# A leaky ReLU's maximum queued behind the attention's next row maximum, and a smaller TensorE budget for the dense layers in each attention cycle

## The chip, the cores and the metric

One core of a Trainium2 chip runs the whole program. The metric is the device time of one execution in microseconds (us); several runs are given with their median. TensorE is written PE, VectorE DVE, ScalarE ACT, GpSimd POOL and SyncE SP, as in the profile. PE multiplies and writes PSUM; DVE, ACT and POOL work elementwise; POOL does not read PSUM here. Each engine takes its instructions in the order in which the program lists them.

## The reference: what is computed

Attention over 8 batches and 8 heads of 576 positions with 64 features, followed by two dense layers with a leaky ReLU between them. In the attention a score further than tau below its row's maximum gets no weight:

```python
scores = scale * np.matmul(q, k.transpose(0, 1, 3, 2))
thresh = np.max(scores, axis=-1, keepdims=True) - tau
scores = np.where(scores >= thresh, scores, -1e9)
attn = np.exp(scores - np.max(scores, axis=-1, keepdims=True))
x = (attn / (attn.sum(-1, keepdims=True) + 1e-9)) @ v      # to 4608 tokens x 512
h = x @ w_in                                               # 512 -> 2048
g = np.maximum(h, 0.0) + alpha * np.minimum(h, 0.0)        # alpha: one per column
out = g @ w_out                                            # 2048 -> 512
```

## The kernel before, in words

**Attention.** Two heads make a pair, so there are 32 pairs; a pair's queries make nine units of 128 rows, so there are 288 units. The loop at L910 runs one cycle for each unit. In cycle i the engines work on units at different stages. The calls of one cycle, in the order in which they are issued (from cycle 52 on), are: `mask` of unit i (DVE, L461: compares with the threshold and multiplies the exponentials); `scores` of unit i+2 (PE, L426: four matmuls, eight for a pair's fifth unit); `lo_k` and `lo` of unit i-1 (DVE, L526: low parts of the transposes); `turn` and `turn_k` of unit i (PE, L470 and L486: transposes); then the dense layers' share (below); then all that is listed for this cycle in `soon` and `later` (preparations of q, k and v, the products with v at L573, their eviction, reciprocals, results); then a first-layer product, if the cycle has one; then `hi_k` and `hi` of unit i (ACT, L522: high parts of the transposes); and at last `rowmax` (DVE, L441) and `expo` (ACT, L449 and L454) of unit i+2. Engines follow this order by hand: the schedule of PE, ACT, DVE and POOL is manual, and only semaphores make one wait for another. The scores have two PSUM buffers, so `scores` of unit i+2 waits for the mask of unit i. The products with v of a pair fall into the sixth and seventh cycle of the pair and into the second and third of the next (L573).

**Dense layers.** Six of the sixteen column blocks of the hidden layer are done in groups of 256 tokens (18 groups), as soon as the tokens of a batch are there. A group is: a load of x (L200), its split into high and low part (ACT L206, POOL L207), six first-layer products (`layer1`, L219, 12 matmuls each, here "L1"), and 36 second-layer matmuls (`layer2`, L249, here "L2") into two accumulators. After an L1 in cycle i, cycle i+1 calls `prelu` from `later`: ACT copies the product with a sign (L232), DVE takes the maximum of that and slope times the product (L233, which reads PSUM again). Cycle i+2 calls `split_g` (POOL L242 cast, L243 difference). The finished accumulator is copied by ACT (L746) and stored by SP (L747).

How many of these go into a cycle is set by a budget in us, `Mlp.cycle`: what the attention uses of PE in this cycle (0.92, and more where the fifth unit's scores, an extra transpose or a product with v falls in) is taken from `CYCLE`; an L1 costs 1.31 and runs only in cycles without a product with v, an L2 costs 0.216:

```python
self.room = min(self.room, TH3) + CYCLE - used
...
elif slot and not HOLD[0] <= i - total < HOLD[1] and self.room > TH1 and ...:
    l1 = True
    self.room -= 1.31
while self.l2 and self.l2[0][0] <= i and ... and self.room > TH2:
    self.step_l2(i)
    self.room -= 0.216
```

The transposes, the products with v, the L1 products and the L2 accumulators share four PSUM buffers (pool `ps_m`, tag "pm").

**Behind the loop.** At cycle 297 the attention's memory is given back. What is left of the queued L2s runs, then the groups that are left, one after another, as `jobs`: `first_layer` (L1056) and `second_layer` (L1068), with `fetch_x` (L866) for their tokens. After that come the other ten column blocks by another method (from L1106 on: products at L1239 and L1417).

Of the kernel before, what the change touches and what calls it, by code (L numbers as in the profile page):

```python
# [15 lines left out]
AF = mybir.ActivationFunctionType  # L16
ALU = mybir.AluOpType
# [8 lines left out]
F1 = 6  # L26
G1 = 256
# [9 lines left out]
GB = 11  # L37
# [15 lines left out]
ACTO, SPLO, PUTO = 1, 2, 1  # L53
# [9 lines left out]
DEC0, DEC = -3, 3  # L63
DECO0, DECO = 16, 3
RDY = 13
CYCLE = 2.6
EW0, EW = 62, 10


# [12 lines left out]
def tile_masked_attention_moe(  # L82
# [11 lines left out]
    nc = tc.nc  # L94
# [14 lines left out]
    turn_sb = const.tile([P, NF], F32, name="turn_sb")  # L109
    tiny_sb = const.tile([P, NF], F32, name="tiny_sb")  # L110
    slope_sb = const.tile([P, NF], F32, name="slope_sb")
# [82 lines left out]
    def load_x(pool, t0, n, gn, bufs):  # L194
        xl = pool.tile([P, NCC, gn], F32R, tag="xl", name=f"xl{gn}_{t0}", bufs=bufs)
        t = t0
        while t < t0 + n:
            b, o = divmod(t, S)
            m = min(S - o, t0 + n - t)
            nc.sync.dma_start(f(xl[:, :, t - t0 : t - t0 + m]), xs[b][:, :, o : o + m].rearrange("c p t -> p c t"))  # L200
            t += m
        return xl

    def split_x(pool, xl, t0, n, gn, bufs):
        xh = pool.tile([P, NCC, gn], F32R, tag="xh", name=f"xh{gn}_{t0}", bufs=bufs)
        nc.scalar.activation(xh[:, :, :n], f(xl[:, :, :n]), AF.Copy)  # L206
        nc.gpsimd.tensor_tensor(xl[:, :, :n], f(xl[:, :, :n]), f(xh[:, :, :n]), op=ALU.subtract)  # L207
        return xh, xl

    def layer1(ps_m, fc, n, x, name):  # L210
        return layer1_into(ps_m.tile([P, 512], F32, tag="pm", name=f"ph{name}"), fc, n, x)
# [13 lines left out]
                )  # L225
        return ph

    def prelu(pool, gn, fc, n, ph, name, bufs):

        t = pool.tile([P, gn], F32, tag="pt", name=f"pt{name}", bufs=bufs)  # L230
        col = slice(fc, fc + 1)
        nc.scalar.activation(t[:, :n], ph[:, :n], AF.Copy, scale=turn_sb[:, col])  # L232
        nc.vector.scalar_tensor_tensor(  # L233
            t[:, :n], ph[:, :n], slope_sb[:, col], t[:, :n], op0=ALU.mult, op1=ALU.max
        )
        return t

    def split_g(g, t, n, eng=None):
        if eng is None:
            nc.scalar.activation(g[:, 0, :n], t[:, :n], AF.Copy)  # L240
        else:
            eng.tensor_copy(g[:, 0, :n], t[:, :n])  # L242
        nc.gpsimd.tensor_tensor(g[:, 1, :n], t[:, :n], f(g[:, 0, :n]), op=ALU.subtract)  # L243
# [7 lines left out]
    fcs1 = list(range(F1))  # L251
# [6 lines left out]
    mem = SimpleNamespace(mp1=None)  # L258
# [374 lines left out]
            nc.sync.dma_start(xs[self.b][self.hp], self.x)  # L633

    pairs = [Pair(pi) for pi in range(npairs)]
    soon, later = {}, {}

    def at_cycle(i, fn, *a):
        later.setdefault(i, []).append((fn, a))
# [5 lines left out]
    for p in pairs:  # L645
        o = 9 * p.pi
        n = o - 9
# [36 lines left out]
    class Mlp:  # L684
# [16 lines left out]
        def step_l1(self, i):  # L701
            gi, st, fi = self.l1.popleft()
            t0, n = groups1[gi]
            if fi is None:
                st["xr"] = load_x(mem.mp1, t0, n, G1, 1)
                at_cycle(i + XO, lambda: st.update(x=split_x(mem.mp1, st["xr"], t0, n, G1, 1)))
                self.gap = i + XO + 2
                return
            name = f"a{gi}_{fi}"
            self.live += 1  # L710
            ph = layer1(ps_m, fcs1[fi], n, st["x"], name)

            alone = i >= total

            def act(ph=ph):
                st[fi] = prelu(mem.mp1, G1, fcs1[fi], n, ph, name, 3)

            def spl():
                g = mem.mp1.tile([P, 2, G1], F32R, tag="g", name=f"g{name}", bufs=GB)
                split_g(g, st.pop(fi), n, None if alone else dict(p=nc.gpsimd, v=nc.vector).get(SPG))  # L720
                st["g"][fi] = g

            at_cycle(i + ACTO, act)
            at_cycle(i + SPLO, spl)
            if fi == F1 - 1:
                for o in range(0, n, P):
                    for fj in range(F1):
                        self.l2.extend((i + L2O, gi, st, o, fj, ti) for ti in range(3))
# [22 lines left out]
        def cycle(self, i, used, slot):  # L751

            self.room = min(self.room, TH3) + CYCLE - used
            l1 = False
            if self.l1 and i >= self.gap and self.live < GB:
                if self.l1[0][2] is None:
                    self.step_l1(i)
                elif slot and not HOLD[0] <= i - total < HOLD[1] and self.room > TH1 and ("i", fcs1[self.l1[0][2]]) in ready:
                    l1 = True
                    self.room -= 1.31  # L760
            while self.l2 and self.l2[0][0] <= i and self.l2[0][4] in self.l2[0][2]["g"] and ("o", fcs1[self.l2[0][4]]) in ready and self.room > TH2:
                self.step_l2(i)
                self.room -= 0.216
            return l1
# [5 lines left out]
    def unit(i):  # L770
        return (pairs[i // 9], i % 9) if 0 <= i < total else (None, 0)

    def do(i, name):
        p, u = unit(i)
        if p is not None:
            getattr(p, name)(u)
# [120 lines left out]
    with tc.manual_schedule(engines=ENGINES) if ENGINES else ExitStack():  # L897
# [12 lines left out]
        for i in range(-3, total + CLOSE):  # L910
            if i == -1:
                p.prep_vh()
                p.prep_vl()
            if i == SPC:
                sp.close()
                mem.mp1 = p1.enter_context(tc.tile_pool(name="mp1", bufs=1, side="right", reuse_waits="tile"))
            do(i, "mask")
            do(i + 2, "scores")
            ab = i < SW
            if not ab or i % 2 == 0:  # L920
                do(i - 1, "lo_k")
                do(i - 1, "lo")
            else:
                do(i + 1, "rowmax")
                do(i + 1, "expo")
            do(i, "turn")
            do(i, "turn_k")
            while nready < len(groups1) and sum(groups1[nready]) <= (i - RDY) // (9 * NPAIR) * S:
                mlp.ready(nready)
                nready += 1  # L930
            used = 0.92
            if unit(i + 2)[1] == 4:
                used += 0.49
            if unit(i)[1] in (1, 3, 4, 6, 8):
                used += 0.11
            used += busy.get(i, 0.0)
            if i >= total:
                used = 0.0
            l1 = mlp.cycle(i, used, i not in busy)
            for fn, a in soon.pop(i, []) + later.pop(i, []):  # L940
                fn(*a)
            if l1:
                mlp.step_l1(i)
            do(i, "hi_k")
            do(i, "hi")
            if ab and i % 2:
                do(i - 1, "lo_k")
                do(i - 1, "lo")
            if not ab or i % 2:
                do(i + 2, "rowmax")  # L950
                do(i + 2, "expo")

        i = total + CLOSE
        at.close()
        left = [ExitStack() for _ in range(7)]
        pool = lambda k, name, side: left[k].enter_context(tc.tile_pool(name=name, bufs=1, side=side, reuse_waits="tile"))
# [66 lines left out]
        jobs = []  # L1023
        for gi, st, fi in mlp.l1:
            if not jobs or jobs[-1].gi != gi:
                t0, n = groups1[gi]
# [4 lines left out]
        for gi in range(nready, len(groups1)):  # L1031
            t0, n = groups1[gi]
# [4 lines left out]
        def fetch(num):  # L1037
            if num < len(jobs) and not jobs[num].x:
                job = jobs[num]
                job.x = fetch_x(job.t0, job.n, i, 4, job.name)  # L1040
# [15 lines left out]
        def first_layer(job, j):  # L1056
            fc = fcs1[j]
            name = f"{job.name}_{fc}"
            while "x" not in job.x:
                cycle()  # L1060
            ph = ps_2.tile([P, 512], F32, tag="ph", name=f"ph{name}", bufs=4)
            layer1_into(ph, fc, job.n, job.x["x"])
            cycle()
            t = prelu(mem.mp1, G1, fc, job.n, ph, name, 3)
            job.g[j] = mem.mp1.tile([P, 2, G1], F32R, tag="g", name=f"g{name}", bufs=GB)
            split_g(job.g[j], t, job.n)

# [21 lines left out]
        pending = None  # L1089
        for num, job in enumerate(jobs):  # L1090
            fetch(num + 1)
            last = num == len(jobs) - 1
            for k, j in enumerate(job.todo):
                if k == 0 and num == 1 and pending.begun:
                    cycle()
                    second_layer(pending, mem.mp1)
                first_layer(job, j)
                if k == (GB - F1 - 1 if last else 0) and num > 0 and not (num == 1 and pending.begun):
                    second_layer(pending, mem.mp1)
            if not last:  # L1100
                pending = job


# [417 lines left out]
```

## Time and profile before

| | |
|---|---|
| median of three runs | 1427.89 us (1427.32 to 1430.94) |
| the profiled execution | 1431.79 us |
| its span, first to last instruction | 1429.6 us |
| PE clock granted, mean | 0.986 of full |
| busy share of the span: PE, DVE, ACT, POOL | 92%, 79%, 70%, 48% |

The span is what the views below are cut from. "Busy" of PE includes modelled ends of pipelined matmuls. A row of a timeline has the start (us from the span's start), the duration in us, the engine, the line, the operation, what it writes and reads, the shape, the number of merged instructions, and in brackets the idle time of the engine before it with what ended it.

### The profile page before, as it was taken

How to read it: one execution, taken by the hardware profiler on the slowest of the kernel's cores; microseconds unless marked ns; L12 is line 12 of the kernel's file. 1: busy time of each engine (PE TensorE's matmuls, PEld its weight loads, DVE VectorE, ACT ScalarE, POOL GpSimd, SP SyncE). 2: the span in 40 equal slices, each digit the busy share in tenths (PEclk: the TensorE clock that was granted, in tenths of full speed). 3: DMA queues.
4: the chain of work that ended last, by engine and by line, in shares of the span. 5: the costliest groups of instructions: out<-in, count | busy, mean ns of one | idle time of the engine just before them, and what ended most of it. 6: DMA issues, size and time to landing. Idle time of an engine off the chain costs nothing. (4 is left out here: it accounts for less than half of the span.)

```text
span 1429.6 us, 26323 instructions
## 1 busy us (share of the span) xinstructions
PE 1320.5 (92%) x8998; PEld 1224.3 (86%) x8998; DVE 1126.8 (79%) x2127; ACT 997.1 (70%) x2162; POOL 686.6 (48%) x865
## 2 busy tenths in 40 slices
PE   5988899999899899999999998999999999999998
PEld 4656888888788788888888987889999999999998
DVE  6888788888888788888888885546887758787785
ACT  6898788878888887878888885656676666333332
POOL 3775465465555555655555544756665554000000
PEclk9999899999999999999999999998999999999999
DMA  7645444543644644554454432335555465656552
GB/s 229 176 123 136 129 132 130 159 124 111 181 117 132 171 125 125 144 161 136 119 162 129 117 103 81 108 111 168 172 188 170 155 197 194 188 170 202 175 162 74
DMA packets 147765, 210.31 MB, mean 147 GB/s; under 512 B 16336, under 2 KB 91888, under 8 KB 147632
## 3 DMA queue, kind: packets, MB, share of 16 engines
q1 hardware_dynamic: 147632, 208.63, 49.8%
q8 instruction: 72, 1.18, 0.3%
q14 instruction: 61, 0.50, 0.1%
HBM read 111.75 MB, written 54.67 MB: 116 GB/s over the span
## 5 line engine op out<-in xcount | busy, mean ns | idle before, releaser
L441 DVE TENSOR_REDUCE nmx<-s 128x1 f32<-128x576 f32 x288 | 216.3, 751 | 62.7 <-PE s L426 60.1
L426 PE MATMUL s<-kh,qst 128*128 128x288 f32 x640 | 149.2, 323 | 86.6 <-DVE p L461 57.9
L449 ACT ACTIVATE p<-s,nmx 128x576 f32<-128x576 f32 x256 | 189.9, 742 | 43.2 <-DVE nmx L441 42.6
L461 DVE SCALAR_TENSOR_TENSOR p<-s,thr,p 128x576 f32<-128x576 f32 x256 | 206.9, 808 | 3.5 <-ACT thr L454 3.0
L426 PEld LDWEIGHTS s<-kh,qst 128*128 128x128 f32 x640 | 98.9, 192 | 127.7 <-issue 54.0
L470 PE MATMUL t<-ident,p 128*128 128x128 f32 x1024 | 156.7, 276 | 1.1 <-DVE p L461 1.1
L249 PE MATMUL acca<-wo,ga 128*128 128x512 f32 x504 | 147.3, 414 | 1.2 <-POOL ga L243 1.2
L219 PE MATMUL pha<-xh,wi 128*128 128x256 f32 x672 | 140.3, 292 | 2.1 <-DVE pta L233 1.7
L1239 PE MATMUL pX<-xh,wa 128*128 128x384 f32 x480 | 136.1, 343 | 6.4 <-DVE pZ L1279 3.9
L426 PE MATMUL s<-kl,qst 128*128 128x288 f32 x640 | 134.1, 300 | 0.0
L1417 PE MATMUL pX<-wb,gh 128*128 128x256 f32 x720 | 129.7, 282 | 0.0
L470 PEld LDWEIGHTS t<-ident,p 128*128 128x128 f32 x1024 | 127.8, 143 | 1.4 <-DVE p L461 1.3
L219 PEld LDWEIGHTS pha<-xh,wi 128*128 128x128 f32 x672 | 111.2, 193 | 6.0 <-DVE pta L233 4.0
L1417 PEld LDWEIGHTS pX<-wb,gh 128*128 128x128 f32 x720 | 111.6, 191 | 0.0
L573 PE MATMUL av<-eo,vst 128*128 128x322 f32 (+1 forms) x512 | 108.6, 335 | 0.0
L861 ACT ACTIVATE gh<-gr 128x1280 fp32r<-128x1280 f32 x45 | 57.4, 1275 | 71.4 <-PE pX L1417 42.7
L526 DVE TENSOR_TENSOR eo<-t,eo 128x512 fp32r<-128x512 f32 (+1 forms) x168 | 97.4, 593 | 10.1 <-ACT eo L522 9.6
L426 PEld LDWEIGHTS s<-kl,qst 128*128 128x128 f32 x640 | 102.8, 192 | 0.0
L1417 PE MATMUL pX<-wb,gl 128*128 128x256 f32 x360 | 101.6, 282 | 0.0
L249 PEld LDWEIGHTS acca<-wo,ga 128*128 128x128 f32 x504 | 89.1, 191 | 14.2 <-POOL ga L243 1.6
L1239 PEld LDWEIGHTS pX<-xh,wa 128*128 128x128 f32 x480 | 90.0, 192 | 8.3 <-DVE pZ L1279 5.3
L219 PE MATMUL pha<-xl,wi 128*128 128x256 f32 x336 | 95.5, 284 | 0.0
(206 smaller groups left out, 3810.6 us busy)
## 6 DMA issues: line engine op xcount, KB each, us to landing
gd<-c SPq DMA_DIRECT2D x90, 192.0 KB
gr<-gd SPq DMA_DIRECT2D x24, 640.0 KB
kr<-in_k_dram SPq DMA_DIRECT2D x31, 320.0 KB
rb<-rvd SPq DMA_DIRECT2D x64, 144.0 KB
xs<-xa SPq DMA_DIRECT2D x32, 288.0 KB
pin<-part SPq DMA_DIRECT2D x18, 512.0 KB
out_dram<-pin SPq DMA_DIRECT2D x18, 512.0 KB
vr<-in_v_dram SPq DMA_DIRECT2D x28, 320.0 KB
```

Source lines behind the costliest of these rows:

```text
L219: nc.tensor.matmul(ph[:, :n], w[:, c, :], xx[:, c, :n], start=(c == 0 and ti == 0), stop=(c == NCC - 1 and ti == 2),)
L249: nc.tensor.matmul(acc[:m, :], gg[:, g, o : o + m], w, start=(first and ti == 0), stop=(last and ti == 2))
L426: nc.tensor.matmul(ps[:, h, :288], w, kk[:, a + h * 288 : a + (h + 1) * 288], start=(ki == 0 and i == 0), stop=(ki == 1 and i == n - 1),)
L441: nc.vector.tensor_reduce(self.nmx[:, j : j + 1], self.S[u][0][:, :, :288], axis=AX.XY, op=ALU.max, negate=True)
L449: nc.scalar.activation(pj, ps[:, :, :288], AF.Exp, bias=nmx[:, j : j + 1], scale=1.0)
L461: nc.vector.scalar_tensor_tensor(pj, ps[:, :, :288], thr[:, j : j + 1], pj, op0=ALU.is_ge, op1=ALU.mult, accum_out=self.sm[:, c : c + 1])
L470: nc.tensor.transpose(tb[:, c, :], pt[:, j, j * D + c * P : j * D + (c + 1) * P], ident)
L526: nc.vector.tensor_tensor(dst[1], ps, f(dst[0]), op=ALU.subtract)
L573: nc.tensor.matmul(pa[:m, :n], w, x, start=(part == 0 and c == 0), stop=(part == z.parts[-1] and c == NKC))
L861: nc.scalar.activation(dst, src, AF.Copy)
L1239: nc.tensor.matmul(ph[:, :H1], a, x[:, c], start=(fresh and c == 0 and ti == 0), stop=(c == 1 and ti == 2), skip_group_check=not fresh,)
L1417: nc.tensor.matmul(acc[:, tb * H2 : (tb + 1) * H2], g[:, pr, tb * P : (tb + 1) * P], w, start=(fresh and n == 0 and ti == 0), stop=(n == l ...
```

## The change

`prelu` is divided: the copy on ACT stays where it was, in the list of the next cycle; the maximum on DVE goes to a new list, `last`, which is run at the end of that cycle, behind `rowmax` and `expo` of unit i+2. In the jobs behind the loop copy and maximum follow each other as before. `CYCLE` falls from 2.6 to 2.4. A variable that had the name `last` is renamed `final`.

```diff
-CYCLE = 2.6
+CYCLE = 2.4
...
-    def prelu(pool, gn, fc, n, ph, name, bufs):
+    def prelu_copy(pool, gn, fc, n, ph, name, bufs):
 
         t = pool.tile([P, gn], F32, tag="pt", name=f"pt{name}", bufs=bufs)
-        col = slice(fc, fc + 1)
-        nc.scalar.activation(t[:, :n], ph[:, :n], AF.Copy, scale=turn_sb[:, col])
+        nc.scalar.activation(t[:, :n], ph[:, :n], AF.Copy, scale=turn_sb[:, fc : fc + 1])
+        return t
+
+    def prelu_max(t, fc, n, ph):
         nc.vector.scalar_tensor_tensor(
-            t[:, :n], ph[:, :n], slope_sb[:, col], t[:, :n], op0=ALU.mult, op1=ALU.max
+            t[:, :n], ph[:, :n], slope_sb[:, fc : fc + 1], t[:, :n], op0=ALU.mult, op1=ALU.max
         )
-        return t
...
-    soon, later = {}, {}
+    soon, later, last = {}, {}, {}
...
             def act(ph=ph):
-                st[fi] = prelu(mem.mp1, G1, fcs1[fi], n, ph, name, 3)
+                st[fi] = prelu_copy(mem.mp1, G1, fcs1[fi], n, ph, name, 3)
+                last.setdefault(i + ACTO, []).append(lambda: prelu_max(st[fi], fcs1[fi], n, ph))
...
             if not ab or i % 2:
                 do(i + 2, "rowmax")
                 do(i + 2, "expo")
+            for fn in last.pop(i, []):
+                fn()
...
-            t = prelu(mem.mp1, G1, fc, job.n, ph, name, 3)
+            t = prelu_copy(mem.mp1, G1, fc, job.n, ph, name, 3)
+            prelu_max(t, fc, job.n, ph)
```

## Rows read from the trace of the kernel before

**Rows 1.** Page, part 1: busy us of each engine, share, instructions.
```profile
PE 1320.5 (92%) x8998; PEld 1224.3 (86%) x8998; DVE 1126.8 (79%) x2127; ACT 997.1 (70%) x2162; POOL 686.6 (48%) x865
```

**Rows 2.** Windows by stage: length, then busy us (instructions) of the engines, clock, DMA.
```profile
core 0: us, PE busy (x) PEld busy (x) DVE busy (x) ACT busy (x) POOL busy (x), PEclk, DMA share, GB/s
159.50:847.20 687.70, 632.23 (x4468) 585.56 (x4468) 581.56 (x1292) 566.98 (x1336) 382.92 (x484) 0.99 0.50 136
890.86:961.02 70.16, 67.88 (x433) 60.99 (x432) 32.56 (x60) 39.04 (x103) 45.69 (x58) 1.00 0.39 123
```

**Rows 3.** Waits, 159.5 to 847.2 us: total us, times, longest.
```profile
PE s L426 <- DVE p L461: 41.1, 54, 2.3
DVE pta L233 <- ACT pta L232: 37.0, 50, 1.9
ACT p L449 <- DVE nmx L441: 36.8, 60, 1.9
```

**Rows 4.** Timeline of DVE, cycle 108.
```profile
333.37 0.21 DVE L592 RECIPROCAL rv<-rv 128x9 f32<-128x9 f32 x1
334.43 0.48 DVE L233 SCALAR_TENSOR_TENSOR pta<-pha,slope_sb,pta 128x256 f32<-128x256 f32 x1 [0.84 <-ACT pta L232]
334.83 0.75 DVE L441 TENSOR_REDUCE nmx<-s 128x1 f32<-128x576 f32 x1
335.49 0.81 DVE L461 SCALAR_TENSOR_TENSOR p<-s,thr,p 128x576 f32<-128x576 f32 x1
```

**Rows 5.** Timeline of PE, cycles 108 and 109.
```profile
332.91 0.43 PE L426 MATMUL s<-kl,qst 128*128 128x288 f32 x2
...
336.37 0.53 PE L426 MATMUL s<-kh,qst 128*128 128x288 f32 x2 [0.93 <-DVE p L461]
336.74 0.43 PE L426 MATMUL s<-kl,qst 128*128 128x288 f32 x2
...
337.46 0.95 PE L249 MATMUL acca<-wo,ga 128*128 128x512 f32 x3
```

**Rows 6.** Timeline of ACT, cycle 108.
```profile
333.94 0.46 ACT L232 ACTIVATE pta<-pha,turn_sb 128x256 f32<-128x256 f32 x1
```

**Rows 7.** Windows: seven L1 and 36 L2 behind the loop, ten L2 in it.
```profile
910.88:920.81 9.93, 9.93 (x85) 9.93 (x84) 4.23 (x8) 5.36 (x14) 6.35 (x10) 1.00 0.42 137
920.81:929.00 8.19, 8.19 (x38) 6.76 (x37) 5.33 (x9) 5.52 (x16) 5.83 (x8) 1.00 0.11 39
...
357.84:360.23 2.39, 2.39 (x13) 1.96 (x12) 2.39 (x7) 1.91 (x5) 1.70 (x4) 1.00 0.92 230
```

**Rows 8.** Windows: pairs 11, 12 and 13, cut where their first scores start.
```profile
299.63:326.90 27.27, 26.22 (x185) 24.07 (x184) 23.07 (x52) 23.18 (x56) 16.41 (x20) 1.00 0.58 151
326.89:354.04 27.15, 24.59 (x184) 23.17 (x183) 22.66 (x53) 22.23 (x55) 15.25 (x21) 1.00 0.46 133
354.04:380.24 26.20, 25.88 (x173) 23.27 (x172) 22.08 (x49) 22.27 (x53) 12.57 (x16) 1.00 0.62 167
```

**Rows 9.** Windows: second cycles with two and with five L2.
```profile
198.18:200.97 2.79, 2.79 (x22) 2.70 (x22) 2.65 (x7) 1.53 (x5) 0.24 (x1) 1.00 1.04 242
...
362.60:366.45 3.85, 3.77 (x25) 3.20 (x25) 2.75 (x6) 2.28 (x7) 0.98 (x2) 1.00 0.88 207
```

**Rows 10.** Timeline of PE behind the attention's last unit.
```profile
886.41 4.61 PE L249 MATMUL acca<-wo,ga 128*128 128x512 f32 x19 [1.15 <-POOL ga L243]
```

**Rows 11.** Windows: the last pair's stretch.
```profile
847.20:872.60 25.40, 20.30 (x144) 18.21 (x143) 22.33 (x51) 19.17 (x48) 5.82 (x8) 1.00 0.10 35
```

**Rows 12.** Line L233, 159.5 to 847.2 us: who waited for it (us, times).
```profile
  PEld pha L219: 4.0, 9
  PE pha L219: 1.7, 4
```

**Rows 13.** Timeline, cycle 197: the end of a max and a weight load.
```profile
604.31 0.48 DVE L233 SCALAR_TENSOR_TENSOR pta<-pha,slope_sb,pta 128x256 f32<-128x256 f32 x1 [0.49 <-ACT pta L232]
...
604.84 0.19 PEld L219 LDWEIGHTS pha<-xh,wi 128*128 128x128 f32 x1 [0.18 <-DVE pta L233]
```

More of the change, by code (lines that the diff above doesn't have):

```diff
@@ L1091, in tile_masked_attention_moe @@
             fetch(num + 1)
-            last = num == len(jobs) - 1
+            final = num == len(jobs) - 1
             for k, j in enumerate(job.todo):
@@ L1097, in tile_masked_attention_moe @@
                 first_layer(job, j)
-                if k == (GB - F1 - 1 if last else 0) and num > 0 and not (num == 1 and pending.begun):
+                if k == (GB - F1 - 1 if final else 0) and num > 0 and not (num == 1 and pending.begun):
                     second_layer(pending, mem.mp1)
-            if not last:
+            if not final:
                 pending = job
```

## The prediction

> **What bounds the kernel now.** I read the page first and then the stretches of the span, because a share over 1429.6 us mixes stages with different limits. The page gives PE 92% and DVE 79% [rows 1]. By stages [rows 2], the attention loop with the dense layers in it (159.5 to 847.2 us, pairs 6 to 30) has PE busy for 632 of 688 us, DVE for 582 and ACT for 567. After the loop come dense layers alone (890.9 to 961.0): PE 67.9 of 70.2, so PE is the bound there. The rest, to the end, the change does not touch.
>
> What the reader is to see is that the loop is not bound by one engine. In it the score matmuls wait 41.1 us in 54 waits for the mask on DVE, the max (L233) waits 37.0 us in 50 waits for its copy from ACT, and ACT's exponential waits 36.8 us for the row maximum [rows 3]. One cycle shows how these hang together. In cycle 108 the scores end at 333.34 and DVE is free at 333.58 [rows 4, 5], but the next instruction in its queue is the max, whose copy ACT ends at 334.40 (333.94 + 0.46) behind two preparations of q [rows 6]. The max runs at 334.43, the row maximum at 334.83, the next mask at 335.49 [rows 4], and the next scores start at 336.37 after PE has waited 0.93 [rows 5]. The row maximum needed nothing of the max.
>
> **The change part by part.** It is two edits, a new order on DVE and a smaller budget. An L1 below is one first-layer product (12 matmuls), an L2 one second-layer matmul; a cycle's place in its pair is the number of its unit modulo nine, counted from first to ninth.
>
> *The budget.* Worked through by the code's own arithmetic, cycle by cycle, 2.6 puts 84 L1 and 504 L2 (14 groups) ahead of the loop's end and 2.4 puts 78 and 447 there. In cycles 52 to 276, up to the last pair, it is 80 and 457 against 72 and 394. Cycles with eight or more L2 go from 13 to 1. Price of the pieces: 84 matmuls or seven L1 take 9.93, so 1.42 each; 36 L2 take 8.19 after the loop, 0.23 each, and 10 in the loop 2.39, 0.24 each [rows 7].
>
> Term 1, the loop gets lighter by 8 L1 and 63 L2. Upper bound at PE's full price: 8 x 1.42 + 63 x 0.239 = 26.4. Lower bound from three neighbouring pairs, which hold 3 L1 and 24 L2, 4 and 12, 1 and 36, and take 27.27, 27.15 and 26.20 [rows 8]: solved for two prices, an L1 costs 1.19 and an L2 0.11, so 8 x 1.19 + 63 x 0.11 = 16.4. I take 25, near the upper end: of the 63, 32 leave the second cycles (64 there now, 32 after), and a second cycle takes 2.79 with two L2 and 3.85 with five [rows 9], 0.35 each.
>
> Term 2, what was moved is paid later. The thirteenth of the groups goes behind the loop: 6 x 1.42 + 8.19 = 16.7, in a stretch where PE has no room, and two more L1 of the group before it stand in the tail: 2 x 1.42. Together +19.5. Its copies, its max, GpSimd's cast and difference, two evictions and their DMAs go along, and a later group's load is four DMAs of SP's queue in place of the loop's; ACT (39.0), DVE (32.6) and POOL (45.7) have room in those 70.2 us [rows 2], so they cost nothing; without that room GpSimd's last difference of the group would show, as the 1.15 in the tail now [rows 10].
>
> Term 3, 27 L2 move into the last pair (38 in cycles 277 to 286 for 11): 27 x 0.239 = 6.4 at most, 0 at least. PE is free there for 5.1 us of 25.4 [rows 11], in pieces, so I take +2.5.
>
> *The order.* Per cycle nothing is added or removed; the max is queued behind the row maximum of the same cycle.
>
> Term 4, first cycles (those after an L1 in a ninth cycle; 17 under the new budget). In cycle 108 the row maximum would run at 333.58, the max still at 334.43 and the mask at 334.84 instead of 335.49: 0.65 gained. If ACT's exponential, no longer waiting, lets the copy come earlier too, the whole wait of 0.93 goes. I take 0.8: 17 x 0.8 = -13.6.
>
> Term 5, the other places outside second cycles (36, of which 10 are in term 7). The 80 maxes wait for 37.0 us; if the 19 in first cycles of now wait like the one of cycle 108 (0.84), that is 16, and the other 61 wait 0.34 each on average. I give PE half back: 26 x 0.17 = -4. Bounds for terms 4 and 5 together: 0, and 41.1, all waits for the mask.
>
> The max is now late itself. Who waits for it? On POOL the cast of g, which feeds L2s several cycles later: 0. Queued behind it on DVE is the next mask, in either order: 0. And PE, because the max frees a PSUM bank. Four banks are shared by the transposes, the value products, the L1 products and the second layer's accumulator; while the accumulator is open, three go round. So an L1 product's bank is wanted two banks later: by the L1 of a ninth cycle that follows an L1 in the eighth, and by the value product of a second cycle that follows an L1 in the first. The first sort shows now: 9 waits of weight loads for L233, 4.0 us [rows 12]; the second (10 places) shows none.
>
> Term 6, second cycles. Take cycle 109 [rows 5]: scores end at 337.17, PE reaches its L2s at 337.46. From engine to engine it takes 0.05 (the max that ends at 604.79 lets a weight load go at 604.84 [rows 13]). So 0.05 to the row maximum, 0.66 from it to the next DVE instruction [rows 4], 0.48 for the max and 0.05 back to PE give 338.41. So the value product waits 0.95 less 0.24 for each L2 ahead of it. The new budget has 18 such places: 12 with one L2, 5 with two, 1 with four: 12 x 0.71 + 5 x 0.47 = +10.9. Bounds: 0, if DVE is ahead and the scores are short, and 17, at 0.95 each.
>
> Term 7, ninth cycles. There are 10, nine with no L2 ahead: 0.95 each, +9.3, less the 4.0 paid now. But the cycle loses the mask's wait as in term 5, and DVE, while PE stands, gets ahead for the first cycle. Between -3 and +5 I take 0.
>
> Sum: -25 + 19.5 + 2.5 - 13.6 - 4 + 10.9 + 0 = -9.7. The profiled execution took 1431.8 (span 1429.6 and 2.2 around it), so it would be 1422.1; it lies 3.9 above the median of the runs, 1427.9, which becomes **1418**. A measurement of this kernel can tell about 0.3%, 4.3 us, from no change.
>
> **A rule against the change.** The row: in the loop PE is busy for 92% of the stretch and DVE for 85%, behind it PE for 97% [rows 2]. The Trainium skill ("Perfetto Trace Analysis", section "Optimization Strategy") says that where the most-contended engine changes over time, interleaving the regimes may help; this change takes a group out of the interleaving. By that rule the L2s were nearly free in the loop and are paid in full after it.
>
> **The rivals.**
> *Not relieved (0.20).* The loop's pairs give back only the pair prices, term 1 is 16.4: the sum is -1.1, 1427. For it: pairs with very different loads differ by 1.1 us of 27. Against it: the three pairs differ also in how their L2s are bunched. It is the rule above, told by rows.
> *The bank instead of the mask: slower (0.20).* One mechanism: the max, last in its cycle, holds the PSUM bank that PE wants next. It pays in full at all 28 places (10.9 + 9.3 - 4.0 = 16.2), and the first cycles gain nothing since the max, late for its copy, still stands ahead of the mask: -25 + 19.5 + 2.5 + 16.2 = +13, 1441. It decides from where the first cycles gain less than 13.2 / 17 = 0.78 each. For it: the waits already there [rows 12]. Against it: in cycle 108 the gain is 0.65 even with the copy as late as now.
> *The waits for the mask vanish (0.14).* Terms 4 and 5 become 36 and the bank waits fall into time that PE has: -25 - 36 + 22 = -39, 1389. For it: most waits for the mask follow a max. Against it: some follow other DVE work, and DVE has 582 busy of 688.
>
> **How the numbers follow.** The forecast has 0.46. Faster: 0.46 + 0.14 and 0.02 of the first rival, 0.62; no change 0.16; slower 0.02 + 0.20, 0.22. Its own range is -4 to -22. The 8 in 10 reach from half way to the fast rival, 1400, to nearly the slow one, 1438.
>
> **What would show it.** Right: 78 L1 copies and 447 + 21 L2 of the pooled accumulator; DVE's idle time before L233 near zero, PE's waits for the mask below 25 us over the loop, the loop's 25 pairs shorter by some 30 us, the stretch behind it longer by about 20. The bank: waits of value products (L573) and of L1s for L233, some 20 in the loop, 11 us or more. Wrong: pairs that stay above 27 us (not relieved), or L233's waits above 25 us (the bank).

## The result and the profile after

| | before | after |
|---|---|---|
| median, first timing | 1429.41 us (4 runs) | 1412.34 us (three runs, 1412.27 to 1417.36) |
| median, timed again on another chip | 1431.65 us (11 runs) | 1413.59 us (4 runs, 1410.99 to 1416.51) |
| ratio to before, first and second timing | | 0.9887 [0.9843, 0.993], 0.9873 [0.9854, 0.9893] |
| the profiled execution, its span | 1431.79, 1429.6 us | 1412.34, 1410.6 us |

The first timing had a fourth run after the change, 3237.63 us, which was disturbed and is left out. The change makes the kernel faster by 1.1 to 1.3%; the medians differ by 17 to 18 us. The forecast was 1418.

First the windows of the profile after, cut as in [rows 2]: the loop's pairs 6 to 30, and what lies between the last scores and the first product of the other method. The second fence is the same stretch behind the loop in the kernel before, for comparison.

```profile
154.61:812.78 658.17, 615.48 (x4310) 560.90 (x4309) 576.90 (x1284) 557.76 (x1324) 370.55 (x466) 0.99 0.51 140
...
833.91:946.13 112.22, 109.63 (x704) 98.71 (x703) 46.55 (x89) 60.96 (x153) 66.37 (x85) 1.00 0.33 105
```

```profile
867.78:961.02 93.24, 88.73 (x565) 79.74 (x566) 41.34 (x79) 50.20 (x129) 57.16 (x73) 1.00 0.36 112
```

Against [rows 2] the loop is 29.5 us shorter. PE's busy time in it fell by 16.8 (632.23 to 615.48) and its idle time by 12.8 (55.5 to 42.7). Behind the loop 19.0 us are added, and PE's busy time there grows by 20.9. All five pieces of the span, each cut at a first matmul (the rows of later runs are read in the same way):

| us | start to pair 6 | pairs 6 to 30 | last pair | last scores to other method | rest |
|---|---|---|---|---|---|
| before | 159.5 | 687.7 | 20.6 | 93.2 | 468.5 |
| after | 154.6 | 658.2 | 21.1 | 112.2 | 464.4 |
| after, second profile | 156.1 | 660.8 | 21.1 | 112.4 | 464.2 |
| difference of the first two | -4.9 | -29.5 | +0.6 | +19.0 | -4.1 |

The same kernel profiled twice differs by 2.6 us in its loop and 1.5 before it; smaller differences than these say nothing.

Then the waits over the loop that answer to [rows 3], with the ones that the change brought (us, times, longest):

```profile
PE s L427 <- DVE p L462: 16.8, 26, 2.2
PEld av L574 <- DVE pta L235: 13.2, 18, 0.8
PEld pha L219 <- DVE pta L235: 12.5, 10, 1.9
PE pha L219 <- DVE pta L235: 10.0, 10, 1.7
PE av L574 <- DVE pta L235: 6.7, 17, 0.5
ACT p L450 <- DVE nmx L442: 6.5, 9, 1.7
DVE pta L235 <- ACT pta L231: 4.2, 13, 0.9
```

The three waits of [rows 3] went from 41.1, 37.0 and 36.8 us to 16.8, 4.2 and 6.5. In their place stand waits for the max, L235: products with v in 18 places and L1 products in 10, 25.7 us on the weight loads (PEld) and 16.7 on the matmuls (PE). [Rows 12] knew only the second kind, 4.0 us on the weight loads and 1.7 on the matmuls.

Cycle 108 is the cycle of [rows 4] to [rows 6]. Here is the timeline of DVE after the change, cycles 108 and 109, and below it PE's:

```profile
324.36 0.22 DVE L593 RECIPROCAL rv<-rv 128x9 f32<-128x9 f32 x1
324.89 0.76 DVE L442 TENSOR_REDUCE nmx<-s 128x1 f32<-128x576 f32 x1 [0.31 <-PE s L427]
325.56 0.47 DVE L235 SCALAR_TENSOR_TENSOR pta<-pha,slope_sb,pta 128x256 f32<-128x256 f32 x1
325.95 0.81 DVE L462 SCALAR_TENSOR_TENSOR p<-s,thr,p 128x576 f32<-128x576 f32 x1
...
328.33 0.47 DVE L235 SCALAR_TENSOR_TENSOR pta<-pha,slope_sb,pta 128x256 f32<-128x256 f32 x1
```

```profile
326.83 0.53 PE L427 MATMUL s<-kh,qst 128*128 128x288 f32 x2
327.19 0.42 PE L427 MATMUL s<-kl,qst 128*128 128x288 f32 x2
...
327.92 0.48 PE L250 MATMUL acca<-wo,ga 128*128 128x512 f32 x1
328.86 0.73 PE L574 MATMUL av<-o,vst 128*128 128x256 f32 x4 [0.46 <-DVE pta L235]
```

The scores of cycle 108 end at 324.85 and the row maximum follows at once, then max and mask without a gap; the mask starts 1.10 after the scores' end, where it took 2.15 (333.34 to 335.49). PE's next scores (326.83) wait for nothing. ACT's copy, which the max had waited for, comes earlier as well: it ends at 325.26, 0.41 after the scores' end, where it ended 1.06 after it (334.40). In cycle 109 the other side shows: the max ends at 328.80 and the product with v starts at 328.86. It had waited 0.46, just the bank's wait that the prediction had put at 0.71 for a place with one L2 ahead.

### The profile page after: what moved, and what is told of

It reads as the page before. It is cut to its first block, busy times and chain, and to the rows that moved or that the text cites. A ratio compares the mean times of both kernels' runs of the same rounds, so it can differ in the third digit from the quotient of the medians.

```text
span 1410.6 us, 26357 instructions
## 1 busy us (share of the span) xinstructions
PE 1321.4 (94%) x8998; PEld 1215.5 (86%) x8998; DVE 1126.3 (80%) x2127; ACT 998.4 (71%) x2173; POOL 685.7 (49%) x860
## 3 DMA queue, kind: packets, MB, share of 16 engines
q8 instruction: 72, 1.18, 0.3%
## 4 chain that ended last, share of the span: by engine, by line
PE 57%; ACT 14%; DVE 13%; issue 6%; DMA 5%; POOL 4%; SPq 1%; ACTq 0%; POOLq 0%; DVEq 0%
PE pX L1422 9%; PE s L427 8%; PE av L574 8%; PE pW L1422 5%; PE pX L1244 5%; PE t L471 4%; PE pha L219 4%; DVE nmx L442 3%; PE acca L250 3%; PE phj L219 3%; DVE p L462 3%; PE pY L1422 2%; ACT p L450 2%; PE pW L1244 2%; PE accj L250 2%
## 5 line engine op out<-in xcount | busy, mean ns | idle before, releaser
L450 ACT ACTIVATE p<-s,nmx 128x576 f32<-128x576 f32 x256 | 190.1, 743 | 14.1 <-DVE nmx L442 13.7
L219 PE MATMUL pha<-xh,wi 128*128 128x256 f32 x624 | 127.3, 288 | 10.3 <-DVE pta L235 10.0
L219 PEld LDWEIGHTS pha<-xh,wi 128*128 128x128 f32 x624 | 102.1, 191 | 14.0 <-DVE pta L235 12.5
L527 DVE TENSOR_TENSOR eo<-t,eo 128x512 fp32r<-128x512 f32 (+1 forms) x168 | 97.4, 593 | 12.1 <-ACT eo L523 10.8
L250 PEld LDWEIGHTS acca<-wo,ga 128*128 128x128 f32 x468 | 83.5, 194 | 12.0 <-POOL ga L244 1.9
L523 ACT ACTIVATE eo<-t 128x512 fp32r<-128x512 f32 (+1 forms) x168 | 84.6, 521 | 12.4 <-PE t L471 11.7
```

The costliest lines, as they stand in the source:

```text
L219: nc.tensor.matmul(ph[:, :n], w[:, c, :], xx[:, c, :n], start=(c == 0 and ti == 0), stop=(c == NCC - 1 and ti == 2),)
L250: nc.tensor.matmul(acc[:m, :], gg[:, g, o : o + m], w, start=(first and ti == 0), stop=(last and ti == 2))
L450: nc.scalar.activation(pj, ps[:, :, :288], AF.Exp, bias=nmx[:, j : j + 1], scale=1.0)
L523: nc.scalar.activation(dst[0], ps, AF.Copy)
L527: nc.vector.tensor_tensor(dst[1], ps, f(dst[0]), op=ALU.subtract)
```

## The experiments

A cycle below is cut at the start of the score matmuls that it issues; "first cycles 71.2" is the sum of all first cycles from cycle 54 to 276. Ratios are to the kernel before on the same chip. The halves and the free bank ran on one chip (before 1432.56, 12 runs); the mixed order, the changed kernel's second timing and the early copy alone on another (1431.65, 11 runs); the last group and the mixed order's second timing on a third (1432.59, 9 runs).

**Each half of the change alone.** The changed kernel with the old budget (`CYCLE = 2.6`):

> The max behind the row maximum, the budget back at 2.6. Theory (the sum of the prediction): the order alone gives back waits for the mask, 19 first cycles by 0.8 us and some 4 us elsewhere, and pays 3 to 5 us of new bank waits (10 second cycles with two to five L2 ahead, 9 ninth cycles with one): about 15 us faster than the kernel before, 1414, loop of pairs 6 to 30 near 673 us (687.7 before), the stretch behind it as before (93 us). Rival 1 (the budget carries the gain): the bank waits eat what the order gives, within 4 us of the kernel before, loop above 684. Rival 2 (the order carries all of it): as the changed kernel or faster, 1412 or less, loop under 672.

The kernel before with the new budget (`CYCLE = 2.4`):

> The budget at 2.4, the max where it was, ahead of the row maximum. Theory (the sum): the loop gets 25 us shorter, the stretch behind it 19.5 longer, 2.5 in the last pair: about 3 us faster, 1426, loop near 663. Rival 1 (the budget carries the gain): 10 us faster or more, loop under 656. Rival 2 (not relieved, what was moved was hidden): 3 us slower or more, loop above 670. In all of them no second cycle waits for a max, and the ninth cycles wait under 5 us.

Measured: the order alone 1415.96, ratio 0.9884 [0.9868, 0.9901], loop 672.8. The budget alone 1426.49, ratio 0.9961 [0.9946, 0.9975], loop 666.6. The window of the loop, order alone, then budget alone:

```profile
154.50:827.26 672.76, 632.25 (x4470) 585.14 (x4469) 583.08 (x1292) 563.00 (x1338) 383.75 (x484) 0.99 0.51 140
```

```profile
155.82:822.42 666.60, 612.73 (x4310) 559.36 (x4309) 575.09 (x1284) 559.66 (x1324) 369.59 (x466) 0.99 0.50 138
```

The two halves do different things. The order leaves PE's work where it was (632.25 against 632.23 before) and takes away 15.0 us of PE's idle time. The budget takes 19.5 us of PE's work out of the loop, and the stretch behind it gets 19.2 longer (112.4). The order alone gives what the whole change gives: the changed kernel, 0.9873 and 0.9887, cannot be told from it. The budget alone gains 0.4%, and on top of the order nothing that these runs can tell.

The order came out as its theory had it (loop near 673, some 15 us faster). The budget's loop came out between its theory (663) and the rival that nothing is relieved (above 670). Its total gained 6 us where 3 were expected; the three pieces that it acts on hold only 1.4 of that in these profiles (-21.1, +0.5 and +19.2). Its last sentence missed: in the old order, too, PE waited for the max at the budget 2.4, in four second cycles (L573) and for more than 5 us in ninth ones (L219). Of the waits of the loop, budget alone:

```profile
PEld pha L219 <- DVE pta L233: 8.9, 10, 1.4
PE pha L219 <- DVE pta L233: 6.1, 8, 1.1
PEld av L573 <- DVE pta L233: 2.2, 4, 0.6
```

| cycles, us | before | budget alone | order alone | after |
|---|---|---|---|---|
| first | 89.1 | 86.0 | 75.5 | 71.2 |
| second | 75.5 | 68.8 | 80.2 | 78.1 |
| third to eighth | 432.4 | 422.6 | 426.4 | 419.5 |
| ninth | 82.8 | 80.5 | 81.8 | 80.7 |

At either budget the order gains 14 to 15 us in first cycles and loses in second ones, 4.7 at 2.6 and 9.3 at 2.4.

**The bank set free.** To take the max off PSUM, it is formed from ACT's copy alone, once at 2.4 and once at 2.6:

```diff
-            t[:, :n], ph[:, :n], slope_sb[:, fc : fc + 1], t[:, :n], op0=ALU.mult, op1=ALU.max
+            t[:, :n], t[:, :n], alpha_sb[:, fc : fc + 1], t[:, :n], op0=ALU.mult, op1=ALU.max
```

> The changed kernel, but the max reads ACT's copy in SBUF alone (alpha times the copy instead of slope times the product), so that the product's PSUM bank is free when the copy ends and no longer when the max ends. Theory (bank waits lie on the path): PE's waits for the max, 16.7 us in 27 waits in the changed kernel, go; the loop shortens by 10 to 16 us (658 to 642 to 648), total about 1402. Rival (they stand in for waits for the mask): PE waits for the mask instead, loop within 4 us of the changed kernel, 1411 to 1415. Rival 2 (a max with two SBUF operands is held up by GpSimd): its mean rises from 0.48 to above 0.7 us and the loop gets longer.

> As the run before in this list (max behind the row maximum, reading SBUF alone), with the budget at 2.6. Theory: as the order alone less its few bank waits, 3 to 6 us faster than that, about 1410; so the smaller budget is worth some 8 us once the bank waits are gone. Rival: with free banks the fuller cycles of 2.6 are as good as or better than 2.4 (the stretch behind the loop is 19 us shorter), 1402 or less.

Measured: 1426.61 and 1440.74 us, 0.9963 [0.995, 0.9976] and 1.0067 [1.0049, 1.0085]: both slower than the same order with the max on PSUM (0.9873 to 0.9887, and 0.9884). At 2.4 no wait for the max is left on PE, second cycles fall from 78.1 to 68.8 and ninth ones from 80.7 to 73.8, so the bank does cost 16 us in the changed kernel. But first cycles go from 71.2 to 89.2 and sixth ones from 75.6 to 81.1. The group of the max, by form (ns shortest, median, longest), and the timelines of DVE, POOL and PE in cycle 108 say why. The fourth of these fences is POOL in the changed kernel, for comparison:

```profile
L235 DVE SCALAR_TENSOR_TENSOR pta<-pta,alpha_sb x72: 467/484/1492, 166.2 to 819.0; 128x256 f32<-128x256 f32 x72
```

```profile
329.32 0.70 DVE L442 TENSOR_REDUCE nmx<-s 128x1 f32<-128x576 f32 x1
330.03 1.40 DVE L235 SCALAR_TENSOR_TENSOR pta<-pta,alpha_sb 128x256 f32<-128x256 f32 x1
331.35 0.80 DVE L462 SCALAR_TENSOR_TENSOR p<-s,thr,p 128x576 f32<-128x576 f32 x1
```

```profile
329.71 1.43 POOL L389 TENSOR_TENSOR qt<-qr,qst 128x576 fp32r<-128x576 f32 x1 [0.59 <-ACT qr L379]
```

```profile
324.97 1.43 POOL L389 TENSOR_TENSOR qt<-qr,qst 128x576 fp32r<-128x576 f32 x1 [0.68 <-ACT qr L379]
```

```profile
332.22 0.53 PE L427 MATMUL s<-kh,qst 128*128 128x288 f32 x2 [1.18 <-DVE p L462]
```

POOL's difference of q ends at 331.14, and the max, begun at 330.03, ends only at 331.43. The mask behind it is late, and PE (last fence) waits 1.18 for it. In the changed kernel the same two overlap in the same cycle (POOL's difference runs from 324.97 to 326.40, the max from 325.56), and the max takes 0.47. 28 of the 72 maxes take over 0.6 us; the excess is 14.1 us in first cycles and 6.0 in sixth ones, against losses of 18.0 and 5.5 there. So the experiment measured the bank's price by cycles, and on the total its second rival came true, the max held up by GpSimd: the mean rose from 0.48 to 0.77 us and the loop got 9.5 longer. At 2.6 both expected times, 1410 and 1402, missed for the same reason (42 of 80 maxes over 0.6 us).

**The max early in second cycles only.** The product with v wants the bank in second cycles, the copy is late in first ones. So the max goes ahead of the row maximum, as in the old order, in second cycles, and behind it elsewhere ("mixed order"). The four expectations are of this at 2.4, of this at 2.6, of the changed kernel timed again, and of the 2.4 kernel timed again on the third chip:

```diff
-                last.setdefault(i + ACTO, []).append(lambda: prelu_max(st[fi], fcs1[fi], n, ph))
+                if (i + ACTO) % 9 == 1:
+                    prelu_max(st[fi], fcs1[fi], n, ph)
+                else:
+                    last.setdefault(i + ACTO, []).append(lambda: prelu_max(st[fi], fcs1[fi], n, ph))
```

> The changed kernel, but a max that falls into a second cycle stands where it stood before, ahead of the row maximum; elsewhere behind it. Theory (the two effects are separate: the order gains in the first cycles, and the max's PSUM bank costs in the second ones): the 18 waits of value products for the max go, second cycles fall from 78.1 to some 69 us (68.8 with the budget alone), first cycles stay near 71; loop 649, total some 9 us below the changed kernel, 1406. Rival (DVE bounds the second cycle in either order): what the value product no longer waits for comes back as waits for the mask, second cycles stay at 76 or more, total 1413 to 1415.

> The same mixed order with the old budget 2.6. Theory (the effects add): against the order alone at 2.6 the second cycles fall from 80.2 to some 75.5, loop 672.8 to 668, total 1411, so 5 us above the mixed order at 2.4: then the budget gains 5 once the bank no longer waits. Rival (the budget's net is nil in any order): both mixed kernels within 2 us of each other.

> The changed kernel again, beside the others on one chip, so that order and budget are compared within one job. If the budget adds nothing to the order: 0.988 to 0.989 of the kernel before, as the order alone had (0.9884). If it adds what the sum of the terms says on top (about 4 us): 0.985 to 0.986. By its first timing: 0.9887.

> The mixed order at 2.4 again, beside the others on one chip, since its first timings were wide (1402.8 to 1414.5). By its first ratio 0.985; by its own cycle sums (loop 12 to 15 us below the changed kernel's) 0.979.

Measured at 2.4: 1410.89, 0.9851 [0.9825, 0.9876], then 1409.43, 0.9822 [0.9798, 0.9847]; at 2.6: 1411.44, 0.9854 [0.9836, 0.9871]. The changed kernel beside the first of these and the one at 2.6: 1413.59, 0.9873, between the two values expected, so whether the budget adds anything to the order stays open. Who waited for the max in the loop, mixed order at 2.4:

```profile
  PEld pha L219: 12.8, 10
  PE pha L219: 10.3, 10
  PEld av L574: 2.1, 4
  PE av L574: 0.5, 2
```

The theory held stage by stage: second cycles 68.9 and 69.0, first ones 70.8 and 71.6, loop 645.7 and 650.6 against the changed kernel's 658.2 and 660.8. Of the products with v that waited for the max, 18 places and 13.2 us on the weight loads, 4 and 2.1 are left, as with the budget alone. So these waits were real time, and DVE did not give them back as waits for the mask (14.2 us in 25). Of the total only 3 to 7 us arrived, not 9, and beside the changed kernel on the same chip the intervals overlap: in these two profiles the start (157.3 and 157.7) took 2 to 3 us more than in the first profile after the change, as profiles differ anyway, and the rest (466.6 and 466.1) 2 more, for which no run here gives the cause. At 2.6 second cycles fell to 74.9 as expected, but the loop (669.6) only by 3.2, since ninth cycles rose from 81.8 to 84.8. Whether 2.4 is better than 2.6 in this order these runs leave open: 0.9851 and 0.9822 against 0.9854.

**The copy earlier instead of the max later.** The kernel before, old order and old budget, with ACT's copy put at the head of its cycle, ahead of the preparations of q. The line moves the whole of `prelu`, so the max too moves up on DVE, ahead of the cycle's reciprocals; it can't start before its copy in either place:

```diff
-            at_cycle(i + ACTO, act)
+            first_at_cycle(i + ACTO, act)
```

> The kernel before (old order, old budget) with one thing new: ACT's copy of the first layer is issued first in its cycle, ahead of the two preparations of q, and not last. Theory (what the old order cost is the late copy, not the max's own 0.48 us): the max finds its copy, its waits for ACT fall from 37 us to under 15, first cycles from 89.1 to some 77, waits for the max's bank do not grow, loop some 13 shorter, total near 1418. Rival (the max costs by standing ahead of the row maximum, whenever its copy comes): first cycles stay above 84, total 1427 or more.

Measured: 1412.08, 0.9867 [0.9848, 0.9885]: as fast as the whole change, from one line. First cycles 77.0, loop 675.7. The waits of the loop, and the timelines of ACT, DVE and PE in cycle 108, which answer to [rows 4] to [rows 6]:

```profile
PE s L426 <- DVE p L461: 25.7, 40, 1.9
DVE pta L233 <- ACT pta L232: 22.6, 49, 1.8
...
PEld pha L219 <- DVE pta L233: 2.2, 8, 0.7
PE pha L219 <- DVE pta L233: 0.4, 1, 0.4
```

```profile
326.17 0.47 ACT L232 ACTIVATE pta<-pha,turn_sb 128x256 f32<-128x256 f32 x1 [0.17 <-PE pha L219]
326.55 0.68 ACT L373 ACTIVATE qst<-qr 128x576 fp32r<-128x576 f32 x1
327.31 0.69 ACT L378 ACTIVATE qr<-qr 128x576 f32<-128x576 f32 x1
```

```profile
326.68 0.48 DVE L233 SCALAR_TENSOR_TENSOR pta<-pha,slope_sb,pta 128x256 f32<-128x256 f32 x1
...
327.41 0.70 DVE L441 TENSOR_REDUCE nmx<-s 128x1 f32<-128x576 f32 x1
328.02 0.81 DVE L461 SCALAR_TENSOR_TENSOR p<-s,thr,p 128x576 f32<-128x576 f32 x1
```

```profile
328.89 0.53 PE L426 MATMUL s<-kh,qst 128*128 128x288 f32 x2
```

The copy now stands before the two preparations, the max still ahead of the row maximum, and the next scores start without a wait that the profile lists (0.93 before). What cost in first cycles was the late copy, not the max's own 0.48 us. Two numbers missed: the total was expected near 1418, and the max's waits for its copy stay at 22.6 us, not under 15. In first cycles DVE's idle time ahead of the max did fall, from 18.5 to 4.0; the largest part of what stays is in ninth cycles (9.2, 9.7 before), which are no longer for it (81.7 against 82.8). Second cycles pay for the early copy: DVE's idle time ahead of the max rose there from 0.7 to 4.6, and they take 77.8 in place of 75.5.

**Early copy with the new budget, and with the mixed order.**

> The kernel before (old order) with ACT's copy issued first in its cycle, and the budget 2.4. Theory (the budget's net is what it is in the old order, 6 us, whatever cures the first cycles): first cycles some 74 us, second 69, loop near 654, total near 1407, 5 us below the early copy at 2.6. Rival (once the first-cycle stall is cured, the budget's gain in the loop equals what it pays behind it): total within 2 us of the early copy at 2.6, 1410 to 1414.

> The changed kernel (budget 2.4) with the mixed order (max ahead of the row maximum in second cycles, behind it elsewhere) and with ACT's copy issued first in its cycle. Theory (order and early copy are two cures for the same first-cycle stall, so they don't add): first cycles stay near 71 us, total within 3 us of the mixed order alone. Rival (each cures a stall of its own): first cycles fall by 10 or more again, total near 1400.

> As the kernel with early copy and mixed order, but with the old budget 2.6. If the cures don't add: the mixed order's time at 2.6, 1411, loop near 669. If they do: first cycles below 68, total near 1402.

Measured: early copy at 2.4 1410.93, 0.9845 [0.9831, 0.9858], loop 651.5. Early copy and mixed order at 2.4 1405.73, 0.981 [0.9786, 0.9835], loop 653.7, first cycles 69.7; at 2.6 1414.62, 0.9872 [0.9852, 0.9892], loop 670.6, first cycles 72.2. Order and early copy don't add: they cure the same stall, as the theory said, and neither 1400 nor 1402 came. With the mixed order the early copy makes second cycles longer, as it did alone: 72.9 against 68.9 and 69.0 at 2.4, 79.7 against 74.9 at 2.6; at 2.4 the weight loads of 11 products with v wait for the max there, against 4. For the budget under the early copy the total lies nearer the rival (1410.93 against 1412.08 on another chip, 0.9845 against 0.9867, with overlapping intervals), while the loop, 24.2 shorter, favours the theory; that stays open. With both cures the budget does gain, 0.981 against 0.9872 on one chip. How much of this is the budget is less sure: the profile at 2.6 ran the stretch behind the loop at a granted clock of 0.95 and took 98.2 us there, 4.4 more than the others at 2.6 with the max on PSUM, which had 1.00. 1405.73 is the best median of the study, below the changed kernel's, and not told apart from the mixed order alone beside it (0.9822).

## Why the prediction was right

Every term has a measurement now. Terms 1 to 3 are read between before and the budget alone or after, terms 4 to 7 between the budget alone and after, which differ by the order only:

| term | forecast | measured |
|---|---|---|
| 1 loop lighter | -25 | -21.1 (loop 687.7 to 666.6) |
| 2 paid behind the loop | +19.5 | +19.0 |
| 3 last pair | +2.5 | +0.6 |
| 4 first cycles | -13.6 | -14.8 (86.0 to 71.2) |
| 5 other places | -4 | -3.1 (third to eighth, 422.6 to 419.5) |
| 6 second cycles | +10.9 | +9.3 (68.8 to 78.1) |
| 7 ninth cycles | 0 | +0.2 (80.5 to 80.7) |
| sum | -9.7 | -9.9 |

The small terms are of the size by which two profiles of one kernel differ: with the changed kernel's second profile, terms 4 to 7 are -14.0, -3.1, +9.3 and +2.0, and the sum is about -7.

- **Term 1** was sized too high; 21.1 is as near to the rival's 16.4 as to the 25. I took 25 of bounds 16.4 and 26.4, because 32 of the L2 leave second cycles at 0.35 each, 11.2; second cycles gave 6.7. PE's busy time fell by 19.5 with the budget alone and its idle time by no more than 1.6.
- **Terms 2 and 3**: the stretch behind the loop paid PE's full price, as was read from [rows 2], which show no room there. The last pair took its 27 L2 nearly for nothing.
- **Term 4** rested on one cycle and held: 0.87 for each of the 17, because the copy came earlier too, the second of the two ways that the term had weighed. Its mechanism, the copy behind two preparations of q [rows 6], is the one that the early copy takes away by itself, with 12.1 us in first cycles for 13.6 by the order.
- **Terms 6 and 7**: the waits stand in 18 second and 10 ninth cycles, the places that counting the four banks had given, and the mixed order takes 14 of the 18 away again; the other 4 were there with the budget alone. The ninth cycles cost the same as with the budget alone. What the bank costs there, 6.9 by the kernel whose max leaves it free, was mostly paid in the old order already: 6.1 us of waits on PE with the budget alone, 10.0 after. The 4.0 that the prediction took off was read at the old budget.
- **Outside the sum**: 9.0 of the span's 19.0 are none of the terms. 4.9 lie before pair 6, where the change does nothing; the profile of before was the longest there (159.5, all others 154.1 to 157.8). From 11.1 us on, where the first scores start, its granted clock was 0.95 up to pair 6 and PE was busy for 129.5 us, against 0.99 and 124.6 after the change. 4.1 lie in the last stretch, of which below. The forecast was a change of 9.7, and the medians differ by 17 to 18 us: the terms were right one by one, or near it, but 7 to 8 us of the gain are in no term, and that 1418 is only 4 to 6 too high is in part because the kernel before was timed 1.5 to 4 us above the 1427.89 that the forecast started from. How much of the medians' difference each of the two pieces holds, one profile of the kernel before can't say.

The rival "the bank instead of the mask" failed at its condition: first cycles gained 0.87 each (14.8 over 17), above its 0.78. "The waits vanish" expected 36 from the mask's waits; 24.3 us of them went (3.5 by the budget alone), but the bank's came. "Not relieved" put the loop's relief at 16.4, and it was 21.1. The Trainium skill's rule beside it ("Perfetto Trace Analysis", section "Optimization Strategy": interleave regimes with different bounds) found no support here: with the order unchanged, taking a group out of the interleaving gained 0.4%.

The signs came out as written: 78 copies L231, 468 L2, the max's idle time 4.2 us, the mask's waits 16.8, the loop 29.5 shorter, the stretch behind it 19.0 longer, 28 places of bank waits. One sign was ambiguous: waits for L233 above 25 us were to speak for the bank, and they are 16.7 us on the matmuls but 25.7 on the weight loads, the way [rows 12] counts its 4.0. What decides is the price by cycles, 9.3 us in second ones and 0.2 in ninth ones.

## What to carry to other kernels

When an engine waits at the head of its queue, look first at why the awaited result is late. Here one line that let the producer run ahead of two unhurried instructions was worth as much as the reordering of the consumer, and weight loads waited less for the max's bank than before (2.6 us against 4.0), though second cycles took 2 us more.

An instruction that is queued later also frees later what it reads. Count the buffers of the pool round by round: that gave the new waits by place before any run, and showed where the old order should stay.

Time that a budget takes out of one stage is paid in another; a change with two halves is best timed half by half, since here one half alone was as fast as the two together.

## What the runs showed of the hardware

**A DVE operation with two SBUF inputs beside POOL.** The max takes 0.47 to 0.48 us after the change, with one input in PSUM, also in the 33 of 72 cases in which a POOL instruction of over 1 us runs beside it. With both inputs in SBUF it took up to 1.49, and 27 of the 28 long ones end 0.28 us after the POOL instruction that was running when they began. POOL's difference of q kept its 1.43 us in both cases. The Trainium skill ("SBUF — State Buffer", section "Who interferes with whom") says that a VectorE instruction with two SBUF inputs contends with a GpSimd instruction that reads SBUF, and that one with at most one SBUF input, outside certain two-port modes, does not; the traces agree on both. So here PSUM as an operand was worth more than the bank that it held (23.5 us in first and sixth cycles against 16.2 in second and ninth ones).

**TensorE at half its clock.** The profiles hold short stretches at half clock in several places, in the loop too (285.2 to 288.6 after the change, PEclk 0.50). In the kernel before the longest lies behind the loop. Windows at the start of the last stretch, before and then after (PEclk is the third number from the end):

```profile
966.00:976.20 10.20, 7.72 (x25) 7.21 (x24) 3.21 (x5) 4.94 (x8) 7.70 (x8) 0.50 0.57 166
```

```profile
954.20:957.60 3.40, 3.40 (x12) 3.40 (x11) 1.24 (x2) 1.69 (x3) 3.40 (x5) 0.50 0.34 94
```

Both run at 1.2 of 2.4 GHz, and in both PE had stood just before: in the kernel before for 0.70 and 1.41 us, and again for 2.48 within the stretch; after the change for 0.27 and 3.23. A matmul of this phase (L1239, 128x384) takes 0.52 at the lower level and 0.34 at the higher one. The changed kernel's second profile shows no such stretch there at all (granted clock 1.00 from 939 to 975), so its length is not fixed by the kernel. With the order alone it was 10.2 again and the last stretch 468.8, with the budget alone 6.8 and 467.1. Nor is the last stretch's length set by it alone: early copy and mixed order at 2.4 had none there and took 466.7, the changed kernel's second profile had none and took 464.2. The kernels at 2.6 took 466.3 to 469.1 for the last stretch and those at 2.4 464.2 to 467.1. That the budget shortens it is what these profiles suggest; nothing was run that tests it by itself.
